# Ten wo chunks on chip, zeros in other places, and part of the last w1 stage summed on VectorE

## The chip, the core and the metric

The kernel runs on one core of a Trainium2 chip. It is one launch. The metric is the device time of the whole program in microseconds, the median of several executions; before the change it is 450.8 us (five runs, 448.94 to 454.15). A core has a matrix engine (PE, with a separate row for its weight loads, PEld), a vector engine (DVE), a scalar engine (ACT), a general engine (POOL) and a sync engine (SP). SP and POOL issue the DMA transfers; all transfers run on the core's 16 DMA engines.

## The reference

A decoder of four layers works on a single token: x is one row of 1024 numbers. Attention and MLP alternate, and both kinds share their weights between the two layers of the kind.

```python
x = x + A(layernorm(x)); x = x + B(layernorm(x))
x = x + A(layernorm(x)); x = x + B(layernorm(x))
# A: q = x @ wq; scores over the last W = 4096 of 32768 cached keys, softmax,
#    times the cached values, @ wo.  32 heads of 128, 4 key/value heads
# B: h = x @ w1 + b1; act = h * tanh(softplus(h)); act @ w2.  1024 -> 3584 -> 1024
```

The outputs are x and, for a given grad_out, the gradients of everything but B_x: of x, of the two caches (32768 positions each, of which only the last 4096 have a gradient that is not zero), of wq (1024 x 4096), wo (4096 x 1024), w1 (1024 x 3584), b1 and w2 (3584 x 1024), all in bfloat16. The zeros of the two cache gradients alone are 58.7 MB of the 98.6 MB that are written.

## The kernel before

A single token makes every weight matrix a matrix-vector product, so the kernel is a sequence of passes over the weights. In order: attention forward (called A1), MLP forward (B2), attention forward again (A3), then the second MLP, which is run forward and backward in one pass over w1 (`mlp_turn`, B4), then attention backward (A3), a pass over w2 that serves the second MLP's forward product and the first MLP's backward product at once (`W2Pass.rest`), the first MLP's backward product with w1 (`mlp_bwd_w1`), and attention backward (A1). The outer products that make the weight gradients come last, when all vectors are known.

wq, K, V and the first NR = 9 chunks of wo stay on chip. A chunk of wo is 256 rows, 0.524 MB; there are 16. The other seven chunks, all of w1 (16 chunks of 0.459 MB, or 14 blocks of 0.524 MB in `mlp_turn`) and all of w2 (14 chunks of 0.524 MB) are loaded anew for each pass into NB = 6 stream buffers, tag `st` of the pool `strm`. A load is issued by SP as soon as its buffer is free, and SP issues in program order: a load that waits for its buffer holds back every later one. The seventh wo chunk of a pass always has to wait for one of the six buffers. In the second forward attention the order of the chunks is the first streamed one, the nine kept ones, the other six (line 541); in the backward attentions the seventh is loaded inside `T` (line 807).

A backward attention needs wo @ g. For the kept chunks 0 to 7 the product runs on rows of the kept, already transposed copy (line 835); the ninth uses `bwd_rows2`. For each streamed chunk half of the rows are transposed on PE (`xpose`), copied back and multiplied, and half are summed on VectorE against g broadcast over the partitions (line 813, g in PSUM as `gbc`, made by `bcast_row`). Each `xpose` puts up to eight transposes into a PSUM tile and copies them out; `evac` gives the copy to VectorE or ScalarE by a running estimate of both. `fill` transposes pieces of wo, V, K and wq in place where PE has time, in that order of the keys; these copies are needed later.

`mlp_bwd_w1` does a full transpose of each w1 chunk (14 blocks of 128 columns) and 14 products, the products one chunk behind the transposes (`pipe`).

The zeros are 112 transfers of 0.524 MB from one tile of zeros, `zt`. `bg_zeros(n, after)` puts a small copy on POOL that waits for the vector `after`, and n zeros behind it; POOL's queue is in order and at most eight of its transfers are outstanding. `zeros(n)` puts them on SP's queue. The table `Z` (line 1133) says how many go where: 3 near the end of the first w2 pass, 16 in the second forward attention, 5, 2, 1, 2, 1, 2 and 6 at the seven blocks of `mlp_turn`, 6 and 26 in the first backward attention, 3 at the last w1 stage, 3 at the start and 36 (on SP) in the last backward attention.

`warm(n)` issues n matmuls of no use whose result is thrown away. `hooks` places pieces of the coming w2 pass into gaps of the layer norm's backward step: "copy" after the copy of the row, "sel" after the sums that follow, "ln" after the norm's sum.

## Time and profile before

| | us |
|---|---|
| median of 5 runs | 450.8 (448.94 to 454.15) |
| the profiled execution, its own time | 449.98 |
| its span in the profile | 447.9 |
| PE, DVE, ACT, POOL busy | 321.8, 236.8, 225.0, 56.8 |
| moved by the DMA engines | 172.25 MB, mean 385 GB/s |

The span is what the profile covers; the remaining 2.1 us lie around it. Busy times are per engine and overlap. The page's second part cuts the span into 40 slices of 11.2 us and gives for each the share of busy time of every engine, the clock of PE (PEclk, in tenths of full speed), the busy share of the DMA engines and the GB/s that they moved. The third part lists the DMA queues: q1 is SP's, q0 is POOL's. The trace can also be asked for the same figures in any other stretch, for the instructions in order of time, and for the transfers in a stretch with their packet sizes. In the timeline an instruction's line holds its start, its time, the engine, the line of the kernel, the operation, what it writes and reads, and in brackets how long the engine had been idle before it and what ended that.

### The profile page before, as it was taken

Reading aid. Unit: us, or ns where it says so; the run is one execution under the profiler, and the core shown is the slowest. Engines: PE = TensorE matmul, PEld = TensorE weight load, DVE = VectorE, ACT = ScalarE, POOL = GpSimd, SP = SyncE. Lnnn points to the kernel's source line nnn. Section 1 sums busy time; section 2 is a strip of 40 time slices with the busy share of each in tenths; the row PEclk is TensorE's granted clock in tenths of the full one; section 3 lists DMA queues with packets and bytes.
Section 4 is the critical chain, followed back from the end, with each engine's and each line's share of the span. In section 5 each row is a group of like instructions: output and inputs, shape, how many; then the busy total and the mean of one; then the engine's idle time right before and its main releaser. Section 6 shows DMA issues by size and latency. Waiting matters only on the chain.

```text
span 447.9 us, 11941 instructions
## 1 busy us (share of the span) xinstructions
PE 321.8 (72%) x5107; PEld 216.7 (48%) x5107; DVE 236.8 (53%) x489; ACT 225.0 (50%) x262; POOL 56.8 (13%) x146
## 2 busy tenths in 40 slices
PE   0556755488997989977799688778868669897400
PEld 0333524387466979954797677754531111121000
DVE  3134201187332756773265855483259889999600
ACT  1121200075241857875493454445329899989600
POOL 2000000001431311341341020052010000000000
PEclk9998555578876999998798589999785555555555
DMA  8999998999999998999999899999999999999994
GB/s 319 393 409 423 409 409 297 408 343 324 417 415 393 395 376 301 384 412 415 416 415 404 320 330 370 341 367 418 416 416 419 419 416 417 418 417 420 416 417 169
DMA packets 52257, 172.25 MB, mean 385 GB/s; under 512 B 5200, under 2 KB 12396, under 8 KB 51180
## 3 DMA queue, kind: packets, MB, share of 16 engines
q1 hardware_dynamic: 41120, 131.61, 75.4%
q0 software_dynamic: 11040, 39.86, 22.2%
q8 instruction: 40, 0.66, 0.6%
q14 instruction: 13, 0.11, 0.1%
q10 hardware_dynamic: 44, 0.01, 0.0%
HBM read 72.89 MB, written 98.58 MB: 383 GB/s over the span
## 4 chain that ended last, share of the span: by engine, by line
PE 20%; ACT 13%; DMA 8%; issue 5%; DVE 4%; POOL 1%; DVEq 0%; ACTq 0%; SPq 0%; POOLq 0%
PE ops L229 6%; DMA w_c<-in_B_w_dram 6%; PE tps L193 6%; ACT wq_b L148 6%; PE acc L229 3%; ACT wo_b L148 2%; DMA wo_c<-in_A_wo_dram 2%; ACT st_o L148 2%; ACT K L148 2%; ACT wo_c L148 1%; PE d L229 1%; DVE K L145 1%; PE tps L623 1%; ACT V L148 1%; PE sm L229 1%
## 5 line engine op out<-in xcount | busy, mean ns | idle before, releaser
L138 POOL DMA_DIRECT2D out_dram<-zt x76 | 40.6, 537 | 44.4 <-DMA out_dram<-zt 41.9
L229 PEld LDWEIGHTS <-w_c 128*128 128x128 bf16 x1120 | 35.8, 101 | 18.9 <-DMA w_c<-in_B_w_dram 14.5
L633 ACT COPY w_c<-tps 128x1024 bf16<-128x1024 bf16 x28 | 28.3, 1012 | 21.6 <-PE tps L623 12.0
L229 PE MATMUL ops<-V 2*128 2x512 bf16 (+1 forms) x160 | 34.8, 598 | 5.9 <-ACT wq_b L148 3.4
L647 DVE CUSTOM_DVE_ANT_0 scr<-w_c,gbc 128x1024 bf16<-128x1024 bf16 x28 | 34.2, 1221 | 5.4 <-DMA w_c<-in_B_w_dram 3.4
L145 DVE CAST wq_b<-ops 128x1024 bf16<-128x1024 f32 (+1 forms) x31 | 33.8, 1149 | 3.8 <-PE ops L229 3.2
L148 ACT CAST wq_b<-ops 128x1024 bf16<-128x1024 f32 (+1 forms) x33 | 33.7, 1138 | 2.2 <-PE ops L229 2.0
L148 ACT COPY K<-tps 128x1024 bf16<-128x1024 bf16 x19 | 18.6, 1029 | 28.4 <-PE tps L193 28.4
L229 PE MATMUL ops<-wo_b 2*128 2x512 bf16 x120 | 23.3, 567 | 10.9 <-ACT wq_b L148 7.2
L229 PEld LDWEIGHTS <-V 128*128 128x128 bf16 (+2 forms) x416 | 14.0, 100 | 27.8 <-issue 27.6
L229 PE MATMUL q<-wq_b,nA_pair 128*32 128x512 bf16 x128 | 11.6, 447 | 16.8 <-DMA wq_b<-in_A_wq_dram 16.8
L623 PE MATMUL tps<-ident_bf,w_c 128*128 128x128 bf16 x224 | 22.3, 260 | 0.6 <-DMA w_c<-in_B_w_dram 0.6
L148 ACT COPY w_b<-tps 128x1024 bf16<-128x1024 bf16 x20 | 19.5, 1015 | 5.5 <-PE tps L193 4.7
L145 DVE COPY K<-tps 128x1024 bf16<-128x1024 bf16 x13 | 8.8, 689 | 24.9 <-PE tps L193 23.0
L229 PEld LDWEIGHTS <-wo_b 2*128 2x128 bf16 (+1 forms) x152 | 5.6, 99 | 29.2 <-issue 28.6
L813 DVE CUSTOM_DVE_ANT_0 wo_c<-wo_c,gbc 128x1024 bf16<-128x1024 bf16 x14 | 16.4, 1218 | 6.0 <-DMA wo_c<-in_A_wo_dram 4.3
L193 PE MATMUL tps<-ident_bf,w_c 128*128 128x128 bf16 x224 | 16.4, 231 | 4.2 <-DMA w_c<-in_B_w_dram 4.2
L229 PE MATMUL acc<-a_pair,w_c 128*128 128x16 bf16 x448 | 15.6, 171 | 5.1 <-DMA w_c<-in_B_w_dram 5.0
L148 ACT COPY w_c<-tps 128x768 bf16<-128x768 bf16 (+1 forms) x14 | 11.6, 830 | 14.7 <-PE tps L193 13.7
L148 ACT CAST K<-ops 128x1024 bf16<-128x1024 f32 x18 | 17.7, 1014 | 2.5 <-PE ops L229 1.8
L193 PE MATMUL tps<-ident_bf,wq_b 128*128 128x128 bf16 x256 | 17.6, 235 | 1.5 <-issue 1.5
L148 ACT COPY wq_b<-tps 128x1024 bf16<-128x1024 bf16 x16 | 15.2, 1043 | 6.6 <-PE tps L193 6.6
(323 smaller groups left out, 660.8 us busy)
## 6 DMA issues: line engine op xcount, KB each, us to landing
out_dram<-zt POOLq DMA_DIRECT2D x76, 512.0 KB, 10.6
out_dram<-zt SPq DMA_DIRECT2D x36, 512.0 KB, 8.5
wo_c<-in_A_wo_dram SPq DMA_DIRECT2D x28, 512.0 KB, 7.8
w_c<-in_B_w_dram SPq DMA_DIRECT2D x32, 448.0 KB, 6.6
w_c<-in_B_w_dram SPq DMA_DIRECT2D x28, 512.0 KB, 6.8
out_dram<-wq_b SPq DMA_DIRECT2D x17, 512.0 KB, 11.5
wq_b<-in_A_wq_dram SPq DMA_DIRECT2D x16, 512.0 KB, 11.8
out_dram<-K SPq DMA_DIRECT2D x8, 1024.0 KB, 12.8
```

The source lines that it names most:

```text
L138: nc.gpsimd.dma_start(zero_jobs.pop(0), zt[:])
L145: nc.vector.tensor_copy(out_ap, in_ap)
L148: nc.scalar.copy(out_ap, in_ap)
L193: nc.tensor.transpose(ps[:, b, :], ap, ident_bf[:])
L229: nc.tensor.matmul(out_ap, lhsT=lhsT, rhs=rhs, start=start, stop=stop, skip_group_check=True, **kw)
L623: nc.tensor.transpose(self.ps[c][:, b, :], w[:, 1, b * P:(b + 1) * P], ident_bf[:])
L633: nc.scalar.copy(self.w[c][:, 1, :], self.ps.pop(c)[:].rearrange("p b c -> p (b c)"))
L647: nc.vector.tensor_tensor_reduce(out=scr[:], in0=w[:, 0, :], in1=gbc[:], scale=1.0, scalar=0.0, op0=ALU.mult, op1=ALU.add, accum_out=self. ...
L813: nc.vector.tensor_tensor_reduce(out=w[:, 0, :], in0=w[:, 0, :], in1=gbc[:], scale=1.0, scalar=0.0, op0=ALU.mult, op1=ALU.add, accum_out=w ...
```

## The change

NR goes from 9 to 10, so ten chunks of wo stay on chip and six are streamed. The room comes from smaller helpers: the tile of zeros is halved and read twice by a broadcast, the matrix of 1/D becomes a column that is broadcast, the pattern matrix `pat` is replaced by four narrow matmuls with `fold`, the replicated q and do columns are kept once instead of four times, and two small tiles share a place with others. The second forward attention takes its first three streamed chunks before the kept ones. `Z` is written anew, with two new places in the first MLP, several in one w2 pass, and one in the second w2 pass. In the first MLP the broadcast of g is made after four w1 chunks instead of before the first. In the last w1 stage columns 0 to 1023 of each even chunk are no longer transposed and multiplied on PE; VectorE multiplies them with dh, broadcast over the partitions in PSUM, and sums them. The hooks get warm matmuls and one w2 chunk less.

```diff
-NR = 9
+NR = 10
...
-    onesD = keep.tile([P, P], FP32, name="onesD")
-    nc.vector.memset(onesD[:], invD)
+    ones1 = keep.tile([P, 1], FP32, name="ones1")
+    nc.vector.memset(ones1[:], invD)
+    onesD = ones1[:, 0:1].to_broadcast([P, P])
...
-    zt = keep.tile([P, ZC], BF16, name="zt")
+    zt = keep.tile([P, ZC // 2], BF16, name="zt")
     nc.gpsimd.memset(zt[:], 0.0)
+    zt2 = zt[:, None, :].to_broadcast([P, 2, ZC // 2])
...
-                zero_jobs.append(zflat[:, i * ZC:(i + 1) * ZC])
+                zero_jobs.append(zflat[:, i * ZC:(i + 1) * ZC].rearrange("p (a b) -> p a b", a=2))
...
-            nc.sync.dma_start(zero_jobs.pop(0), zt[:])
+            nc.sync.dma_start(zero_jobs.pop(0), zt2)
...
+    def over_groups(out, rhs, start, stop):
+        for c in range(NC):
+            mm(out[32 * c:32 * c + 32, :], fold[:], rhs, start, stop, tile_position=(0, 32 * c))
...
-        nc.vector.tensor_copy(tt[:, 0:TD], dn_ps)
+        if more is None:
+            nc.vector.tensor_copy(tt[:, 0:TD], dn_ps)
+        else:
+            nc.vector.tensor_add(tt[:, 0:TD], dn_ps, more)
...
-        order = early + late if first else late[0:1] + early + late[1:]
+        order = early + late if first else late[0:3] + early + late[3:]
...
-            if not first and i == 0:
-                held[NO - 1] = wo_load(NO - 1)
...
-        gbc = bcast_row(g_bf)
         for i in range(2 * TD):
             t, hf = i // 2, i % 2
             w = w1_load(i)
+            if i == 4:
+                gbc = bcast_row(g_bf)
+                bg_zeros(Z["B2a"], n_bf)
...
+        def blocks(i):
+            return range(8 if i % 2 == 0 else 0, NW2)
+
         def T(i):
             w = w1_load(i)
             ws[i] = w
-            xpose(*alt_blocks(w[:, 0:1024], 4))
+            if i % 2:
+                xpose(*alt_blocks(w[:, 0:1024], 4))
             xpose(*alt_blocks(w[:, 1024:1792], 3))
...
+        def V(i):
+            if i % 2 == 0:
+                ev[0] += 1.3
+                nc.vector.tensor_tensor_reduce(out=ws[i][:, 0:1024], in0=ws[i][:, 0:1024], in1=big[0][:], scale=1.0, scalar=0.0,
+                                               op0=ALU.mult, op1=ALU.add, accum_out=tw[:, i // 2:i // 2 + 1])
...
-        pipe(list(range(2 * TD)), T, M)
-        return ln_bwd(nacc.cols(0, TD), sv["n32"], sv["rstd"], g_col, lname, nxt)
+        rep8 = work.tile([P, TD, P], BF16, name="rep8", tag="kp")
+        nc.vector.tensor_copy(rep8[:], sv["dh_bf"][:, 0:TD, None].to_broadcast([P, TD, P]))
+        T(0)
+        top("two")
+        big.append(pools["top"].tile([P, D], FP32, name="dhbc"))
+        for k in range(TD):
+            o = (k // 2) * 2 * P + k % 2
+            mm(big[0][:, o:o + 2 * P - 1:2], rep8[:, k, :], ident_bf[:], k % 4 == 0, True)
+        V(0)
+        for i in range(1, 2 * TD):
+            T(i)
+            V(i)
+            M(i - 1)
+        M(2 * TD - 1)
+        return ln_bwd(nacc.cols(0, TD), sv["n32"], sv["rstd"], g_col, lname, nxt, tw[:])
...
-        bwd_rows2(dacc, wo_kept[NR - 1], NR - 1, g_bf, started=False)
+        for c in range(8, NR):
+            bwd_rows2(dacc, wo_kept[c], c, g_bf, started=c > 8)
...
-    Z = dict(B2=3, A3=16, B4=[5, 2, 1, 2, 1, 2, 6], A3c=6, A3d=26, W1=3, A1c=3, A1d=36)
+    Z = dict(B2a=2, B2={0: 2, NW2 - 2: 3}, A3=17, B4=[1, 2, 2, 2, 2, 2, 3], A3c=6, A3d=24, B4w={2: 2}, W1=4, A1c=3, A1d=37)
...
-    hooks.update(copy=lambda: w2p.tp(0), sel=lambda: w2_ahead([0]), ln=lambda: w2_ahead([1, 2]))
+    def copy_gap():
+        w2p.tp(0)
+        warm(3)
+
+    def sel_gap():
+        w2_ahead([0])
+        warm(2)
+
+    def ln_gap():
+        w2_ahead([1])
+        warm(4)
+
+    hooks.update(copy=copy_gap, sel=sel_gap, ln=ln_gap)
     g2, g2b = attn_bwd(g3, g3b, "A3", sA3, True, "B2")
-    x4, wg2 = w2p.rest(3, g2b, x3, "x_B4", bcast_row(g2b), 0)
+    x4, wg2 = w2p.rest(2, g2b, x3, "x_B4", bcast_row(g2b), Z["B4w"])
```

The new `Z` asks for 114 zeros and there are 112, so the last run on SP has 35.

## The prediction

> **What bounds the kernel now.** I read the page's slices first, because the kernel moves 172 MB and I wanted to know whether the transfers leave any room.
>
> ```profile
> GB/s 319 393 409 423 409 409 297 408 343 324 417 415 393 395 376 301 384 412 415 416 415 404 320 330 370 341 367 418 416 416 419 419 416 417 418 417 420 416 417 169
> ...
> q0 software_dynamic: 11040, 39.86, 22.2%
> ...
> HBM read 72.89 MB, written 98.58 MB: 383 GB/s over the span
> ```
>
> The best slices hold 416 to 420 GB/s; I take 417 as the ceiling, so a 0.524 MB transfer costs 1.26 us where the queues are full. From slice 28 (302 us) to the end all slices but the last are at the ceiling: what counts there is how many bytes are left. Before it are dips, and there the chain of work decides. So I need two accounts: the chain up to the point P where the last w1 stage has written gA_pair (291.9 us), and the bytes after P.
>
> Next, stretches of 2 us around the dips (time; busy us of PE, PEld, DVE, ACT, POOL; PEclk; DMA share; GB/s).
>
> ```profile
> 70.00:72.00 2.00, 1.04 (x15) 1.04 (x16) 0.90 (x3) 0.00 (x0) 0.00 (x0) 0.50 0.54 206
> 72.00:74.00 2.00, 2.00 (x82) 2.00 (x79) 0.00 (x0) 0.00 (x0) 0.00 (x0) 0.50 0.43 61
> 136.00:138.00 2.00, 0.87 (x32) 0.78 (x32) 0.69 (x1) 0.00 (x0) 0.00 (x0) 1.00 1.04 422
> 162.00:164.00 2.00, 0.56 (x16) 0.47 (x16) 0.55 (x1) 0.47 (x1) 0.00 (x0) 1.00 1.09 365
> 172.00:174.00 2.00, 2.00 (x57) 2.00 (x55) 1.71 (x5) 0.31 (x2) 0.00 (x0) 1.00 0.41 154
> ```
>
> At 70 to 74 the six stream buffers are full and the queues empty; at 136 and 162 it is the reverse, full queues and an idle PE; at 172 PE is full and the queues empty. Zeros that sit in the second kind and not in the first are in the wrong place. The timeline names what PE waited for, the seventh streamed wo chunk (139, 202) and a late w1 chunk (286):
>
> ```profile
> 139.15 0.59 PE L229 MATMUL sm<-o_pair,wo_c 128*128 128x16 bf16 x16 [2.27 <-DMA wo_c<-in_A_wo_dram]
> ...
> 202.70 0.62 PE L193 MATMUL tps<-ident_bf,wo_c 128*128 128x128 bf16 x8 [1.41 <-DMA wo_c<-in_A_wo_dram]
> ...
> 286.45 0.96 PE L193 MATMUL tps<-ident_bf,w_c 128*128 128x128 bf16 x14 [1.33 <-DMA w_c<-in_B_w_dram]
> ```
>
> SP's own timeline shows the same seventh load ahead of the last run of zeros:
>
> ```profile
> 289.86 5.75 SPq L348 DMA_DIRECT2D wo_c<-in_A_wo_dram  x2
> 295.66 6.03 SPq L129 DMA_DIRECT2D out_dram<-zt  x4
> ```
>
> **The change, along the chain.** With ten chunks kept, six are streamed, and the six buffers hold all of them: the seventh load, which waited for a buffer and then for the zeros ahead of it, is gone from three stages (three loads of 0.524 MB).
>
> *Second forward attention (112 to 142).* PE's 2.27 us wait goes; its matmuls and the 13 row chunks stay. The seventeenth zero (one more) lies behind, in a queue that is full either way. -2.3.
>
> *Second MLP, forward and back (144 to 190).* PE is 2.00 of 2.00 almost throughout; it idled 0.15 + 1.44 + 0.50 us at 160 to 166 for a w1 block behind ten zeros. The zeros go from 5, 2, 1, 2, 1, 2, 6 to 1, 2, 2, 2, 2, 2, 3: two w1 blocks (1.05 MB at 348 GB/s, 3.0 us) and two zeros (2.5 us) fit in the 6.4 us of a block. I take 1.5 of the 2.1 us. Five zeros fewer leave holes here, which cost the chain nothing. -1.5 (0 to -2.1).
>
> *First backward attention (190 to 242).* The 1.41 us wait goes. Chunk 9 costs 16 products from the kept copy (0.55) where its streamed form cost 8 transposes and 8 products (0.62 + 0.36): -0.4. Against it, two more kept chunk halves were transposed in the MLP's fixed slots, so two K units slide into this stage, 8 transposes at 0.57 to 0.61 each: +1.2. Together -0.7. The three hooks get nine warm matmuls; at full clock 512 columns take about 0.22 us (7 in 1.67 us at 290). Those at "copy" and "sel" stand ahead of the next step on PE, less what the DVE copy hides: +0.65; the four at "ln" take the place of chunk 2's forward products and transposes. The broadcast after them ran at clock 0.50 (1.04 us, 0.62 at full clock), so I give 0.35 back: +0.3.
>
> *First MLP (70 to 110).* Moving the broadcast behind four w1 chunks lets PE start 1.6 us earlier at 70.2; two zeros (2.5 us) enter the hole at 71 to 74.5. The w1 loads then end about when they did; the broadcast (1.03 us) hides beside them, PE being half idle at 76 to 80, and would cost that if it were not. Two zeros at w2's first chunk: DVE sets the pace there (1.22 + 0.08 us each of 14), six buffers ahead; +0.5 for a load that comes late (0 to +2.5).
>
> *Second w2 pass (243 to 264).* Two zeros more, but its backlog is shorter by two zeros and a wo load (3.8 us) against a chain shorter by 0.7. DVE's waits for loads there are 0.17 + 0.77 + 0.68; 0 (-1 to +1.5).
>
> *Last w1 stage (264 to 290).* A pair of chunks cost 28 transposes and 28 products, 2.27 us of PE; now 20 and 20, 1.62. DVE per pair: one 768-column copy (0.56) and the new sum over 1024 columns (1.22 + 0.08, the row of the same operation in the w2 stage) = 1.86; ACT 1.01 + 0.80 = 1.81. At 0.93 us a chunk both lie under the load (0.459 MB, 1.1 us): no engine becomes the bound. What it adds on the path is the broadcast of dh: 0.69 (DVE) + 1.03 (PE), beside the first transposes. Before, the stage took 1.5 us a chunk, with waits for loads that land 6.4 to 7.5 us after issue. Now the loads decide: chunks 6 to 15 (4.6 MB) and four zeros (2.1 MB) from 266.3 take 16.1 us; +2 for landing and +2.4 for the last chunk's transposes, eviction and products make 286.8 against 289.8. Six buffers held 2.4 us each keep it from reaching that: -2.5 (0 to -5). VectorE runs in order: behind each sum stands the next 768-column copy, and PE's products wait for that, with 0.2 us of slack a chunk.
>
> *After P.* From 291.9 to 447.9 it is 156.0 us. One zero fewer remains (38 for 39): -1.26. The wo load: -1.26. SP's zeros no longer stand behind it, up to 5.8 us earlier; the stretches from 290 to 302 lack 0.69 MB against 417 GB/s (1.7 us), of which I take 1.2. -3.7.
>
> Chain -6.2, bytes -3.7. Can the queues follow? Before P 110.4 MB move now (172.25 less 61.8, the stretches after P added up); two wo loads fewer and one zero more make 109.9 MB, 263.6 us at 417, plus 3.3 at the start and 3.7 for the 1 KB rows: 270.6 of 285.7 us. The holes shrink from 20 to 15 us; it can. At no cost: the small sums of the softmax (four narrow matmuls for one of 0.39 us) and the row layouts, which lie where ACT and DVE end at 421 us and the transfers at 441.
>
> **The zeros' source.** It is halved, and a broadcast makes each row two runs of 2 KB instead of one of 4 KB. No row shows 2 KB. The two sides, the w1 blocks (1 KB rows) and the last stores:
>
> ```profile
> DMA packets 1391, 1.39 MB, mean 348 GB/s; under 512 B 46, under 2 KB 1390, under 8 KB 1390
> ...
> DMA packets 1368, 4.99 MB, mean 416 GB/s; under 512 B 150, under 2 KB 150, under 8 KB 1368
> ```
>
> So 1 KB takes 47 ns on a DMA engine and 4 KB 158; a straight line gives 84 for 2 KB, +0.08 us a zero. But 3.5 KB rows (360 to 376 us) hold 416 too, so the surcharge fades before 4 KB. I take half, 0.04: 38 zeros after P, 1.5 us; 47 in the full stretches before it, 1.9, of which 0.5 reaches the chain. +2.0. The ends: none, 0; at the 1 KB price, +0.25 a zero.
>
> [...]
>
> **The sum.** -6.2 - 3.7 + 2.0 = -7.9 on the profiled execution's own 449.98 us (span 447.9 and 2.1 around it): 442. The median is 450.8, so that is 2% faster.
>
> **Rivals.** *More of it:* 2 KB costs nothing and the w1 stage reaches its load rate (-3.0 or better), second w2 pass -1: 449.98 - 6.2 - 3.7 - 1.5 - 2 = 436.5. For it: 3.5 KB rows pay nothing. Chance 0.18. *Only bytes:* the waits return elsewhere (17 zeros ahead of the first w1 blocks, zeros ahead of w2 loads); three loads (3.8 us) go, 2 KB eats 2, 1 KB rows as before: 448, from 446.3 to 453. For it: the w2 loads at 244 took 6.9 us behind zeros. 0.20, most of it within 1%. *The change does not do what it says:* zeros gated at 70 start too late for the hole (the first buffer came free at 72.1 and the rate was back only in 74 to 76, so some 2 us pass from issue to bytes) and lengthen the w1 loads by 2.5: 444.5, within the forecast. *Slower:* zeros at the 1 KB price. The place is the runs where only zeros flow (112 to 140, 200 to 240, 295 on): 85 of the 112 outside the thin stages, 0.25 each, 21 us in place of 2: 461. It decides from 0.12 us a zero (+9%), where 85 zeros eat the 9.9. Against it: the same 4 KB is written in order. 0.12.
>
> Chances: 442 (438 to 446) 0.50, 436 0.18, bytes only 0.20, slower 0.12. Beyond 1%, about what a measurement can tell from no change (446.3 to 455.3): faster 0.69, same 0.19, slower 0.12. The range takes in most of the neighbours on both sides: 435 to 453.
>
> **What would show it.** Zero-only stretches at 417 GB/s (no surcharge), 404 (mine) or 348; no wait for wo_c in the last chunks of any attention stage; no PE hole at the fourth block of the second MLP; 70 to 74 above 300 GB/s; P near 285; the last w1 stage about 25 us from dh to P instead of 27.6, its sums at 1.22 us. It is wrong if P moves by less than 3 us, or if the stretch after P grows.

## The result, and the profile after

The changed kernel takes **455.0 us** (median of 22 runs, 452.3 to 459.0) against 451.2 us of the kernel before in the same comparisons: ratio **1.0082**, 95% interval 1.0057 to 1.0106. It is 0.8% slower where 2% faster was forecast, and 455 lies outside the range of 435 to 453. The profiled execution took 457.31 us, with a span of 455.2. (Of the runs below, the profile of e7 is of an execution in a slower state, at a granted clock of 0.717, so no stage is read from it.)

The page of the changed kernel, the same lines as before:

```profile
GB/s 321 389 414 413 406 408 343 411 389 340 397 401 371 319 336 368 350 361 407 412 373 261 362 286 347 325 374 402 392 380 379 404 405 403 402 406 400 407 407 323
...
q1 hardware_dynamic: 45024, 129.52, 75.0%
q0 software_dynamic: 11184, 40.39, 23.2%
...
HBM read 71.31 MB, written 98.58 MB: 373 GB/s over the span
```

The bytes fell as the sum said (71.31 MB read for 72.89), but the *rate* fell more, to 373 GB/s for 383. Two things are new. From slice 28 on, where only stores are left, all slices but the last stand at 379 to 407 where they stood at 416 to 420. And slices 22 to 26, the second w2 pass and the last w1 stage, run thinner than before: 261 to 362 where they stood at 320 to 404.

The stretches of the prediction, and two new ones at 148 and 248 us (time; busy us of PE, PEld, DVE, ACT, POOL; granted clock; DMA share; GB/s):

```profile
70.00:72.00 2.00, 1.63 (x58) 1.63 (x58) 1.08 (x3) 0.00 (x0) 1.62 (x3) 0.50 0.75 260
72.00:74.00 2.00, 1.68 (x37) 1.59 (x34) 0.00 (x0) 0.00 (x0) 0.72 (x1) 0.50 0.91 235
136.00:138.00 2.00, 2.00 (x37) 0.82 (x30) 0.00 (x0) 0.00 (x0) 0.69 (x1) 0.91 1.00 369
148.00:150.00 2.00, 0.00 (x0) 0.00 (x0) 0.00 (x0) 0.00 (x0) 0.00 (x0) 0.50 1.04 353
162.00:164.00 2.00, 2.00 (x57) 2.00 (x55) 1.56 (x9) 1.71 (x3) 0.00 (x0) 1.00 1.07 400
248.00:250.00 2.00, 1.90 (x56) 1.73 (x53) 1.97 (x3) 1.65 (x3) 0.00 (x0) 1.00 0.50 135
```

The old holes are closed as meant: 61 GB/s became 235 at 72, and PE is full at 136 and at 162. But at 148 PE does nothing at all beside a full queue, and at 248 the queue is half empty beside a full PE. The timeline says what PE waits for at 147 and 150:

```profile
147.02 0.60 PE L231 MATMUL sm<-nB_pair,w_b 128*128 128x16 bf16 x16 [2.75 <-DMA w_b<-in_B_w_dram]
150.46 0.59 PE L231 MATMUL sm<-nB_pair,w_b 128*128 128x16 bf16 x16 [2.85 <-DMA w_b<-in_B_w_dram]
```

The wait for the seventh wo chunk is gone, and its heir is the first w1 block of the turn. The chain can be taken from gate to gate (GpSimd's small copies that release the zeros, the broadcast of g at the start of the second w2 pass, and VectorE's operation that writes dh, the gradient that the first MLP's w1 product needs). The gates at the ends of the table's first, second and fifth row, before and then after:

```profile
112.52 0.19 POOL L136 COPY gate_t<-nA_pair 128x1 bf16<-128x1 bf16 x1 [2.45 <-DVE nA_pair L295]
...
189.72 0.19 POOL L136 COPY gate_t<-gA_pair 128x1 bf16<-128x1 bf16 x1 [5.87 <-DVE gA_pair L321]
...
291.98 0.64 POOL L136 COPY gate_t<-gA_pair 128x1 bf16<-128x1 bf16 x1 [24.38 <-DVE gA_pair L321]
```

```profile
115.79 0.19 POOL L138 COPY gate_t<-nA_pair 128x1 bf16<-128x1 bf16 x1 [2.67 <-DVE nA_pair L301]
...
194.14 0.19 POOL L138 COPY gate_t<-gA_pair 128x1 bf16<-128x1 bf16 x1 [7.92 <-DVE gA_pair L330]
...
300.76 0.64 POOL L138 COPY gate_t<-gA_pair 128x1 bf16<-128x1 bf16 x1 [24.96 <-DVE gA_pair L330]
```

So the chain moved like this:

| stretch | before, us | after, us | forecast | measured |
|---|---|---|---|---|
| start to nA gate (first MLP and before) | 112.52 | 115.79 | +0.5 | +3.3 |
| nA gate to gA gate (second attention, turn) | 77.20 | 78.35 | -3.8 | +1.2 |
| gA gate to second w2 pass | 52.33 | 51.73 | -0.4 | -0.6 |
| second w2 pass to dh | 21.82 | 24.78 | 0 | +3.0 |
| dh to P | 28.11 | 30.11 | -2.5 | +2.0 |
| P to the end of the span | 155.9 | 154.4 | -3.7 and +1.5 | -1.5 |

P is at 300.76 instead of 291.98: +8.8 us for a forecast of -6.2 (and +0.5 of the zeros' price).

### The profile page after: what moved, and what is told of

It is laid out like the page before. It is cut to its first block, busy times and chain, and to the rows that moved or that the text cites. A ratio compares the mean times of both kernels' runs of the same rounds, so it can differ in the third digit from the quotient of the medians.

```text
span 455.2 us, 11790 instructions
## 1 busy us (share of the span) xinstructions
PE 325.7 (72%) x5060; PEld 221.1 (49%) x5060; DVE 237.1 (52%) x491; ACT 227.4 (50%) x264; POOL 72.6 (16%) x150
## 3 DMA queue, kind: packets, MB, share of 16 engines
HBM read 71.31 MB, written 98.58 MB: 373 GB/s over the span
## 5 line engine op out<-in xcount | busy, mean ns | idle before, releaser
L140 POOL DMA_DIRECT2D out_dram<-zt x77 | 56.2, 731 | 33.0 <-DMA out_dram<-zt 27.1
L150 ACT COPY K<-tps 128x1024 bf16<-128x1024 bf16 x20 | 19.4, 1024 | 30.3 <-PE tps L195 30.3
L147 DVE CAST wq_b<-ops 128x1024 bf16<-128x1024 f32 (+1 forms) x29 | 31.7, 1151 | 3.6 <-PE ops L231 3.0
L150 ACT CAST wq_b<-ops 128x1024 bf16<-128x1024 f32 (+1 forms) x31 | 31.7, 1137 | 2.2 <-PE ops L231 2.0
L231 PEld LDWEIGHTS <-V 128*128 128x128 bf16 (+2 forms) x416 | 14.1, 101 | 27.8 <-issue 27.6
L630 PE MATMUL tps<-ident_bf,w_c 128*128 128x128 bf16 x224 | 22.6, 262 | 0.8 <-DMA w_c<-in_B_w_dram 0.8
L150 ACT COPY w_c<-tps 128x1024 bf16<-128x1024 bf16 (+1 forms) x16 | 13.7, 908 | 14.6 <-PE tps L195 10.8
L195 PE MATMUL tps<-ident_bf,K 128*128 128x128 bf16 x256 | 19.5, 236 | 0.0
L195 PEld LDWEIGHTS <-K 128*128 128x128 bf16 x256 | 16.6, 107 | 4.2 <-issue 4.1
```

What stands on the lines that cost most here:

```text
L140: nc.gpsimd.dma_start(zero_jobs.pop(0), zt2)
L147: nc.vector.tensor_copy(out_ap, in_ap)
L150: nc.scalar.copy(out_ap, in_ap)
L195: nc.tensor.transpose(ps[:, b, :], ap, ident_bf[:])
L231: nc.tensor.matmul(out_ap, lhsT=lhsT, rhs=rhs, start=start, stop=stop, skip_group_check=True, **kw)
L630: nc.tensor.transpose(self.ps[c][:, b, :], w[:, 1, b * P:(b + 1) * P], ident_bf[:])
```

## The experiments

Two suspects came out of the two traces. One is the **places** of the zeros: those that now stand ahead of loads. The other is the **rate** of the transfers themselves, which fell even where the bytes and their form are the same. The sum on VectorE is the third thing to settle.

### e1: the old places

```diff
-Z = dict(B2a=2, B2={0: 2, NW2 - 2: 3}, A3=17, B4=[1, 2, 2, 2, 2, 2, 3], A3c=6, A3d=24, B4w={2: 2}, W1=4, A1c=3, A1d=37)
+Z = dict(B2a=0, B2={NW2 - 2: 3}, A3=16, B4=[5, 2, 1, 2, 1, 2, 6], A3c=6, A3d=26, B4w={}, W1=3, A1c=3, A1d=36)
```

> The changed kernel with the zero transfers gated where the kernel before had them (3 at w2 chunk 12, 16 in the second forward attention, 5 2 1 2 1 2 6 in the turn, 26 in the first backward attention, 3 at the last w1 stage, none in the second w2 pass). Theory 'places' (the gain went to zeros that now stand ahead of loads: first MLP +1.7, first w2 pass +1.6, first block of the turn +5.2 against the 4.7 gained before it, second w2 pass +3.0): those waits go, nB gate near 140, start of the second w2 pass 3 to 4 us earlier, P about 294 to 296 instead of 300.8, the time about 449 (ratio to the kernel before about 0.995). Theory 'end of the queue' (what is after P decides, two-run rows and slower stores): P may come earlier, but the queue is full from the start of the last w1 stage on and the time stays within 2 us of 455. Against both: 5 zeros at the turn's first block are more than the 1 of the change; if the sum ahead of that block decides (16 + 5 for 17 + 1), the turn's first block becomes longer still, by 2.5 to 4 us.

Measured: 451.8 us, ratio 0.9985 (0.9950 to 1.0020); the changed kernel's 1.0082 lies outside that. P came at 296.65, 4.1 us earlier. The nA gate is back at 112.52, so the 3.3 us of the first MLP are the zeros at 70 and at w2's first chunk, and nothing else. The turn's first block takes 6.5 us again, but its third took 10.5. The waits of PE from 138 us to the turn's end (us in total, times, longest), the changed kernel and then e1:

```profile
PE sm L231 <- DMA w_b<-in_B_w_dram: 5.6, 2, 2.8
```

```profile
PE sm L231 <- DMA w_b<-in_B_w_dram: 6.1, 4, 4.1
```

In the kernel before it was 2.1. So the hole only moved: zeros issued in the second attention and in the turn meet the w1 loads one block earlier or later.

One wait stayed. E1 puts no zeros into the second w2 pass, and yet the pass took 25.0 us to dh, where the changed kernel took 24.8. VectorE waited there for loads, and when the pass began (243 us) the queue was still full of GpSimd's zeros, at 359 to 381 GB/s from 238 to 248 us:

```profile
253.48 1.22 DVE L654 CUSTOM_DVE_ANT_0 scr<-w_c,gbc 128x1024 bf16<-128x1024 bf16 x1 [1.99 <-DMA w_c<-in_B_w_dram]
...
255.42 1.22 DVE L654 CUSTOM_DVE_ANT_0 scr<-w_c,gbc 128x1024 bf16<-128x1024 bf16 x1 [0.71 <-DMA w_c<-in_B_w_dram]
...
258.90 1.22 DVE L654 CUSTOM_DVE_ANT_0 scr<-w_c,gbc 128x1024 bf16<-128x1024 bf16 x1 [2.25 <-DMA w_c<-in_B_w_dram]
```

### e2: the old last w1 stage

```diff
-        T(0)
...
-        V(0)
-        for i in range(1, 2 * TD):
-            T(i)
-            V(i)
-            M(i - 1)
-        M(2 * TD - 1)
+        pipe(list(range(2 * TD)), T, M)
```

> The changed kernel with the last w1 stage of the kernel before: all 14 blocks of every chunk on TensorE, no sum on VectorE and no broadcast of dh. Theory 'VectorE sum costs' (broadcast 1.9 us at half the granted clock, and a thinner TensorE stage in which the granted clock stays at 0.50): the stage from dh to P shrinks from 29.7 to about 27.6, the granted clock is 1.00 in its second half, the time falls by 1 to 2 us, to 453 to 454. Theory 'loads decide' (my forecast's own step): the stage grows by 1 to 2.5 us with TensorE back at 1.6 us a pair more, time 456 to 458. Third: it makes no difference, under 1 us, because the four zeros and the loads of the stage set its length.

Measured: 456.0 us, ratio 1.0066 (1.0026 to 1.0107): the same as with the sum. From dh to the layer norm's first copy the stage took 27.6 us, with the sum 27.95. In e1, with the sum but three zeros, it took 25.96; the kernel before, without the sum and with three zeros, 25.95. The stage is longer in the kernels with the fourth zero, whichever engine sums. The profiles read here part this way: 24.7 to 26.6 us with three zeros (the kernel before, e1, e4, e6, e8, e9, e11, e14, e15, e16), 27.2 to 27.95 with four (the changed kernel, e2, e3, e5, e13). But the kernels with four also have the other new places, and no run moves that one zero alone.

### e3 and e4: one run of 4 KB, or two of 2 KB

In e3 SyncE's late zeros read a 4 KB row again, from a slot of the stores; in e4 the kernel before gets the halved source, and nothing else.

```diff
 # e3, on the changed kernel
-        slots.extend(cut_up(wo_flat, 8192, (2048,) * (NR - 4)))
+        *sl, zl = cut_up(wo_flat, 8192, (2048,) * (NR - 4))
+        slots.extend(sl)
+        nc.gpsimd.memset(zl, 0.0)
 # e4, on the kernel before
-    zt = keep.tile([P, ZC], BF16, name="zt")
+    zt = keep.tile([P, ZC // 2], BF16, name="zt")      # and zt2, as in the change
```

> The changed kernel whose 35 zeros on SyncE's queue after P read one run of 4 KB a row again, from a buffer of 4 KB that is one store slot fewer (5 slots there, as the kernel before). The zeros that GpSimd issues keep the two runs of 2 KB. Theory '2 KB packets on SyncE's queue cost' (304 to 352 us at 379 to 401 GB/s instead of 416): the packets of that stretch are 4 KB, its rate 415 or more, and the time falls by 3 to 4.5 us, to 451 or 452. Theory 'the whole end is slower for another reason' (the stores behind it too run at 399 to 410 GB/s): the rate stays at 380 to 405 and the time stays within 1 us of 455. By my forecast's price of 0.04 us a zero it would fall by 1.4.

> The kernel before with one edit: the zero source is half as wide and a broadcast makes each row two runs of 2 KB. Theory '2 KB packets on SyncE's queue cost, on GpSimd's not': the 36 zeros after P take 0.1 to 0.13 us more each, the time rises by 3.5 to 4.5 us to 454.5 to 455.5 (ratio 1.008 to 1.010); the stretches where only GpSimd's zeros flow (112 to 140, 205 to 238) keep 415 GB/s and 4 KB packets. By my forecast's price (0.04 a zero, on both queues): +2.0. By the price of 1 KB rows: +20. If the stores after 352 us also fall from 416 to about 405 GB/s here, the slower end of the changed kernel comes with the zeros' form too.

Measured: e3 456.2 us, 1.0081 (1.0048 to 1.0115); e4 453.7 us, 1.0036 (0.9988 to 1.0085), not told apart from no change. E3's windows show why its time says little: the zeros waited for the memset and began 10 us later than in the changed kernel (309.05 for 299.01 us on SyncE's queue), which left a hole.

```profile
304.00:312.00 8.00, 4.72 (x76) 3.70 (x69) 5.02 (x9) 3.26 (x5) 5.25 (x14) 0.83 0.53 208
312.00:320.00 8.00, 6.82 (x95) 4.33 (x97) 1.03 (x5) 5.83 (x8) 2.85 (x18) 0.96 1.02 402
...
384.00:400.00 16.00, 14.09 (x80) 2.94 (x80) 15.04 (x14) 15.28 (x17) 0.00 (x0) 0.50 1.02 402
```

But they also show something I had not thought of: with 4 KB rows the zeros run at 402, not 416, and so do the stores at 384 that no edit touched. In e4, on the other base, zeros of two 2 KB runs hold 404 to 406 GB/s at 304 to 344 and the stores behind them 417 to 419:

```profile
312.00:320.00 8.00, 6.83 (x71) 3.32 (x70) 4.52 (x18) 2.14 (x3) 1.07 (x6) 1.00 1.05 404
...
352.00:368.00 16.00, 9.35 (x53) 1.77 (x52) 13.50 (x14) 13.98 (x14) 0.00 (x0) 0.50 1.03 418
```

Zeros and stores of the kernel before, and then of the changed kernel:

```profile
328.00:336.00 8.00, 4.19 (x44) 2.44 (x37) 3.98 (x13) 2.46 (x3) 1.67 (x6) 0.84 1.03 416
...
352.00:368.00 16.00, 9.58 (x52) 1.81 (x52) 12.75 (x13) 13.93 (x14) 0.00 (x0) 0.50 1.03 418
```

```profile
328.00:336.00 8.00, 6.28 (x137) 3.72 (x134) 0.00 (x0) 1.30 (x3) 0.07 (x1) 0.68 1.04 379
...
352.00:368.00 16.00, 12.10 (x60) 2.40 (x56) 15.66 (x15) 15.18 (x16) 0.00 (x0) 0.50 1.03 403
```

So in e4 two runs of 2 KB cost 3% (404 for 416 GB/s), 0.04 us a zero; and the changed kernel has a second slowness, in transfers of any form, that e4 does not have.

### e5 and e6: 32 bytes

What else differs is where the buffers lie in SBUF. In the kernel before the zero source starts at a multiple of 512 bytes and K and V 256 past one; in the changed kernel these are 32 and 288, and wq and wo are at 64 instead of 32.

```diff
 # e5, on the changed kernel: everything behind lies 32 bytes lower
-    ones1 = keep.tile([P, 1], FP32, name="ones1")
-    eps_t = keep.tile([P, 1], FP32, name="eps_t")
+    one_eps = keep.tile([P, 2], FP32, name="one_eps")
+    ones1, eps_t = one_eps[:, 0:1], one_eps[:, 1:2]
 # e6, on the kernel before: the same with eps_t and sel2
```

> The changed kernel with two small constants (1/D and eps) in one tile, so that every buffer behind them lies 32 bytes lower in SBUF: zero source, K and V at multiples of 64 bytes, wq, wo and the stream buffers at 32 past one, as in the kernel before (in the changed kernel it is the other way round). Nothing else differs. In the profiles the 4 KB packets of SyncE's stores take 159.6 to 161 ns in the kernel before and its two-run variant and 163 to 165 ns in the changed kernel and three variants of it. Theory 'address' (the 64-byte position of the buffers sets the packet time): packets back to about 160, the stretch from 352 us to the end at 416 to 420 GB/s instead of 399 to 410, the V loads at 159, the time falls by 5 to 8 us, to 447 to 450 (ratio 0.985 to 0.997). Theory 'program' (number of slots, order of stores, DRAM placement of the program): packets stay at 163 to 165, time 455 within 1 us.

> The kernel before with two small constants (eps and the row selector) in one tile, so that every buffer behind them lies 32 bytes lower: zero source, K and V at 32 past a multiple of 64 bytes, wq, wo and the stream buffers at multiples of 64, as in the changed kernel. Theory 'address': the store packets of 4 KB go from 160 to 163 to 165 ns, the stores at the end run at about 404 GB/s, the time rises by 6 to 10 us, to 458 to 462. Theory 'program': 160 ns and about 452 as before.

Measured: e5 451.3 us, 0.9990 (0.9959 to 1.0021). One tile less, 32 bytes, and some 4 us are back. P came at 298.1 and the rest took 152.3 us, 2.2 less than in the changed kernel. Its zeros on SyncE's queue run at 403 to 407 GB/s for 379 to 392 (320 to 344 us), its stores at 405 to 420:

```profile
336.00:344.00 8.00, 3.28 (x29) 2.53 (x33) 3.55 (x16) 1.01 (x1) 1.17 (x5) 0.76 1.05 407
...
352.00:368.00 16.00, 11.17 (x60) 2.18 (x58) 14.59 (x15) 14.51 (x14) 0.00 (x0) 0.50 1.03 419
```

But e6 went against the simple form of the theory: 450.1 us, 0.9957 (0.9921 to 0.9994), not slower at all. Its wq loads (at a multiple of 512 there) even became faster, 159 ns a packet for 163, while part of its stores went from 160 ns to between 161 and 165. "The other side of 64 bytes" is not the rule.

### e7, e8, e9: both cures together

e7 has the edits of e1 and e5; e8 besides these the old last w1 stage; e9 is e7 with three zeros moved from the second forward attention to the first backward one (`A3=13`, `A3d=29`).

> The changed kernel with both cures at once: zeros gated where the kernel before has them, and every buffer 32 bytes lower. Theory 'two causes' (places cost about 4 us, the 32 bytes about 4, independent of each other): P near 293 to 295, the stretch after P about 152, time 446 to 448 (ratio 0.985 to 0.993). Theory 'one cause' (both let the same full queue catch up before P): the gains overlap, time 450 to 451.5 as with either alone.

> The kernel with both cures, and the last w1 stage of the kernel before (no sum on VectorE). So far the stage from dh to the layer norm's first copy took 25.95 us (kernel before, 3 zeros, all on TensorE), 25.96 (sum on VectorE, 3 zeros), 27.6 (TensorE, 4 zeros), 27.5 and 27.95 (VectorE, 4 zeros). Theory 'loads and zeros set the stage, whichever engine sums': 26 us again, time within 0.3% of the kernel with both cures. Theory of my forecast (the sum takes 2.5 us off): stage 28 to 28.5, time 2 us longer. Theory 'the sum costs' (a wait for ScalarE's copies in place of the wait for loads): stage 24.5 or less, time 1 to 1.5 us shorter.

> The kernel with both cures, with three zeros moved from the second forward attention (13 for 16) to the first backward one (29 for 26). Theory 'zeros ahead of the w1 loads': in the changed kernel with the old places the third block of the turn took 10.5 us against 4.9 to 5.3, TensorE idle for w1 blocks that stand beside zeros; three fewer ahead of them take 3.8 us off that wait, and three more behind lie over the stretch at 246 to 250 us where the queues run thin. nB gate the same or 1 us earlier, end of the turn 2 to 4 us earlier, P 1.5 to 3 us earlier, time 1.5 to 3 us less than with both cures alone. Theory 'the queue is full anyway': the second w2 pass starts behind three zeros more, P and time within 1 us.

| kernel | us | ratio to the kernel before |
|---|---|---|
| changed kernel | 455.0 | 1.0082 (1.0057 to 1.0106) |
| e1, old places | 451.8 | 0.9985 (0.9950 to 1.0020) |
| e5, 32 bytes lower | 451.3 | 0.9990 (0.9959 to 1.0021) |
| e7, both | 447.2 | 0.9885 (0.9860 to 0.9911) |
| e8, both, no sum on VectorE | 448.1 | 0.9910 (0.9873 to 0.9948) |
| e9, both, three zeros later | 445.6 | 0.9853 (0.9807 to 0.9899) |

The gains add up: 0.0097 and 0.0092 alone, 0.0197 together. So there are two causes, not one seen twice. E9's interval does not part it from e7, but its trace shows the step: the wait for w1 blocks, 6.1 us in e1, is no longer among the turn's waits, and the turn takes 44.9 us from gate to gate (45.6 before, 51.4 changed):

```profile
140.31 0.18 POOL L138 COPY gate_t<-nB_pair 128x1 bf16<-128x1 bf16 x1 [14.21 <-DVE nB_pair L301]
...
185.17 0.19 POOL L138 COPY gate_t<-gA_pair 128x1 bf16<-128x1 bf16 x1 [6.80 <-DVE gA_pair L330]
```

P is at 288.9.

### e10 and e12: loads and zeros alone

Here the offset is measured by itself, without a kernel around it.

```diff
+    for c in range(16):                         # e12: offset 0 everywhere
+        at = 10240 + 2560 * c + (0, 32, 64, 256)[c // 4] // 2
+        nc.sync.dma_start(big[:, at:at + 2048], wo_v[c])
+    for order in (offs, (288, 0, 448, 64, 256, 32, 480, 128, 320, 96, 384, 192)):
+        for o in order:
+            for k in range(4):
+                nc.sync.dma_start(dst.pop(0), big[:, 2560 * k + o // 2:2560 * k + o // 2 + 2048])
```

> No layer is computed and only the zeros are written. Sixteen 4 KB-row loads of wo go to SBUF rows that start 0, 32, 64 and 256 bytes past a multiple of 512 (four loads each), then 96 transfers of zeros with 4 KB rows are issued by SyncE from rows 0, 32, 64, 96, 128, 192, 256, 288, 320, 384, 448 and 480 bytes past a multiple of 512, four each, once in this order and once in another, then sixteen of two 2 KB runs from 0 and 32. Theory 'the 64-byte position of a buffer sets its own packet time': odd multiples of 32 give 163 to 165 ns in both passes, the others 159 to 160, whichever pass; two runs of 2 KB 84 from 0 and 86 to 89 from 32. Theory 'not the buffer's own position' (only the whole kernel's mix of buffers): 159 to 160 throughout, in both passes; then the 32 bytes act through something that this kernel does not have.

> The kernel of loads and zeros alone, with every row at offset 0 (a multiple of 512 bytes), all else the same. In the run with mixed offsets the first 48 stores took 159 ns a packet at every offset, and from the 49th on 161 to 167 with 159 again for offsets 0 and 256 at first. Theory 'destination or time' (the second output, or how long the queue has run): the second half is at 161 to 167 here too. Theory 'offsets, by way of the packets before' (rows off the 512-byte grid bring the engines out of step, rows on it bring them back): 159 to the end, the two-run rows at 84, and 420 GB/s throughout.

The packet records of e10's second pass, mean duration of a 4 KB packet, in the order of issue:

```
offset past 512   288    0   448    64   256    32   480   128   320    96   384   192
ns              161.5  159.0 161.5 163.5 159.0 160.7 163.7 163.9 164.0 163.9 163.9 167.5
```

In the first pass all twelve took 159.0 or 159.1. The loads tell little (159 to 163, the first group with the start of the queue in it). The rates of e10 (time; GpSimd; clock; DMA share; GB/s): first pass, second pass, two runs of 2 KB from offset 32:

```profile
48.00:68.00 20.00, 0.00 (x0) 1.00 1.03 420
...
112.00:132.00 20.00, 0.00 (x0) 1.00 1.02 406
...
160.00:164.00 4.00, 0.00 (x0) 1.00 1.03 381
```

And of e12, the same transfers to the same places with every row at offset 0:

```profile
112.00:132.00 20.00, 0.00 (x0) 1.00 1.03 420
...
160.00:162.00 2.00, 0.00 (x0) 1.00 1.05 409
```

E12 holds 159 ns and 420 GB/s to the end of its 4 KB rows, so neither the destination nor the time slows the queue: the offsets do (each of the two kernels ran once). They don't do it at once, though. Twelve offsets ran at full pace as long as none had slowed; once the queue was slow, only the rows at 0 and 256, the two of the twelve on a grid of 256 bytes, were at 159. Why the price comes late is not shown. Rows of two 2 KB runs ran at 409 GB/s on the grid, for 420 with 4 KB (0.035 us a zero), and at 381 off it, the rate of the changed kernel's late zeros (379 to 381).

In these two runs a start off the grid cost 0 to 4.5% of the rate for 4 KB rows (420 down to 401 GB/s, e10 at 132 to 146 us) and 7% for two runs of 2 KB (409 to 381). What in the transfer takes that time no run shows.

### e11 and e14: the sum on VectorE, in order

e9's waits of PE in this stage, then those of e11, in which the copies are dealt out by hand (of an odd chunk ScalarE 1024 columns and VectorE 768, of an even one ScalarE the 768); e14 is e9 without the sum.

```diff
 # e11, in T(i)
-                xpose(*alt_blocks(w[:, 0:1024], 4))
-            xpose(*alt_blocks(w[:, 1024:1792], 3))
+                xpose(*alt_blocks(w[:, 0:1024], 4), "a")
+            xpose(*alt_blocks(w[:, 1024:1792], 3), "v" if i % 2 else "a")
```

> The kernel with both cures and three zeros moved later, and in the last w1 stage the copies are dealt out by hand: of an odd chunk ScalarE takes the 1024 columns and VectorE the 768, of an even one ScalarE the 768 while VectorE sums. So far ScalarE took both copies of each odd chunk one after the other (1.71 us), TensorE waited for it, and VectorE took the even chunk's. Theory 'the new wait on ScalarE ate the gain': the stage from dh to the next layer's gate goes from 26.85 us to 24.5 to 25.5, the time falls by 1 to 2 us. Theory 'loads set it' : 26.5 to 27, time the same within 0.3%. By my forecast's sum (0.93 us of either engine a chunk, loads of 1.1 us): 24.4 or less.

> The kernel with both cures and three zeros moved later, and the last w1 stage all on TensorE. With both cures the stage from dh to the layer norm took 24.9 us in this form, with the sum on VectorE 26.6, with the sum and the copies dealt out by hand 24.7. Theory 'the sum as written costs': stage near 24.9, time 1 to 2 us less than 445.6. Theory 'the queue evens it out' (a stage that ends earlier finds the transfers no further): time the same within 0.3%, as between the two kernels with both cures (0.9885 and 0.9910).

PE's waits in the stage: the kernel before, e9, and e11 (us in total, times, longest):

```profile
PE tps L193 <- DMA w_c<-in_B_w_dram: 4.2, 5, 1.6
```

```profile
PE acc L231 <- ACT w_c L150: 3.6, 11, 0.7
...
PE tps L195 <- DMA w_c<-in_B_w_dram: 1.2, 2, 1.0
```

```profile
PE tps L195 <- DMA w_c<-in_B_w_dram: 3.3, 3, 1.7
...
PE acc L231 <- ACT w_c L150: 1.3, 3, 0.7
```

The sum: 4.2, 4.8 and 4.6 us. The sum on VectorE does take work off PE, and the wait for loads shrinks; but a wait for ScalarE comes in its place, because the helper that balances the copies gives ScalarE both copies of every odd chunk (1.71 us in a row). With the copies dealt out by hand, most of the wait for loads is back. From dh to the layer norm's copy the stage took 26.6 us in e9, 24.7 in e11, and 25.8 (e14) and 24.9 (e8) with no sum at all. The times don't part: e9 0.9853, e11 0.9884 (0.9805 to 0.9963), e14 0.9876 (0.9793 to 0.9959). The step is worth nothing, in either direction, that these runs can tell.

### e13, e15, e16: which buffers

e13 moves the zero source alone onto a multiple of 512. e15 (on e9) and e16 (on the kernel before) order the buffers so that stream buffers, zero source, wq, wo, K and V all start at multiples of 256; nothing grows.

```diff
 # e15, e16
+    small = ctx.enter_context(tc.tile_pool(name="small", bufs=1))   # x0, eps_t, sel2, neg1: 128 bytes
+    strm = ctx.enter_context(tc.tile_pool(name="strm", bufs=NB))
     keep = ctx.enter_context(tc.tile_pool(name="keep", bufs=1))
     work = ctx.enter_context(tc.tile_pool(name="work", bufs=1))
-    strm = ctx.enter_context(tc.tile_pool(name="strm", bufs=NB))
+    ...                                                             # zt, wq_b, wo_b, K, V first in keep
```

> The changed kernel with the zero source alone 32 bytes lower, on a multiple of 512 (it and the 512-byte identity change places with a 32-byte tile); wq, wo, K, V and the stream buffers stay where the changed kernel has them. Theory 'the zero source': the 35 zeros after P run at 404 GB/s instead of 381 (2.5 us), and the stores behind them, no longer started out of step, at 412 to 420 instead of 399 to 410 (1.5 to 2.5 us more): 450.5 to 452.5, as when all buffers were moved. Theory 'all buffers': zeros at 404, stores still at 399 to 410: 452.5 to 453.5. Theory 'the step is lost anyway': zeros still at 380 to 390, 455.

> The kernel with the old zero places and three zeros later, with its buffers laid out in another order so that the stream buffers, the zero source, wq, wo, K and V all start at a multiple of 256 bytes (nothing grows; in the kernel before zero source, K and V do, in the changed kernel none). In the run of mixed offsets only the groups at 0 and 256 kept 159 ns a packet once the queue had slowed. Theory 'rows on 256 bytes keep the packets short': loads of wq, V and wo at 159 to 160 ns instead of 162 to 164, all stores after P at 159 to 160, 418 to 421 GB/s after the zeros, time 2 to 4 us below the 445.6 of the same kernel 32 bytes lower (ratio 0.975 to 0.982). Theory 'only the zero source counts' : packets of loads and stores as there, time within 1 us of it.

> The kernel before with the same order of buffers, all of them at multiples of 256 bytes; nothing else differs. Theory 'rows on 256 bytes keep the packets short': loads of wq and wo at 159 to 160 ns instead of 163 to 164 (some 12 MB of them ahead of the chain, 0.7 us), stores flat as they are, time 0.5 to 2 us shorter (ratio 0.995 to 0.999). Theory 'only the zero source counts' (it is on 512 already): no change.

Windows of the changed kernel, of e13, and of e15:

```profile
336.00:344.00 8.00, 5.34 (x74) 3.22 (x73) 3.33 (x12) 1.69 (x2) 1.17 (x5) 0.89 1.04 381
...
384.00:400.00 16.00, 14.12 (x84) 2.87 (x78) 15.05 (x14) 15.17 (x17) 0.00 (x0) 0.50 1.02 402
```

```profile
336.00:344.00 8.00, 4.80 (x63) 3.38 (x52) 3.66 (x14) 1.52 (x2) 1.17 (x5) 0.84 1.05 406
352.00:368.00 16.00, 11.81 (x57) 2.32 (x56) 14.73 (x15) 15.18 (x16) 0.00 (x0) 0.50 1.03 419
...
384.00:400.00 16.00, 14.10 (x80) 2.86 (x74) 15.04 (x14) 15.27 (x17) 0.00 (x0) 0.50 1.00 401
```

```profile
44.00:64.00 20.00, 13.52 (x207) 6.86 (x207) 2.58 (x10) 2.18 (x6) 0.00 (x0) 0.52 1.03 418
...
384.00:400.00 16.00, 14.27 (x76) 2.97 (x74) 16.00 (x15) 14.95 (x17) 0.00 (x0) 0.50 1.03 420
```

E13: 453.4 us, 1.0004 (0.9957 to 1.0051), better than the changed kernel. Its zeros hold 406, and the stores from other buffers, still off the grid, start at 419 behind them and fall to 401 later on. So the zero source is part of the 4 us; the rest of e5's gain came with the other buffers, which e5 moved as well. E15: 444.8 us, **0.9809** (0.9767 to 0.9852); e16: 449.1 us, **0.9941** (0.9907 to 0.9975). In both every load of wq, V and wo takes 159 to 161 ns a packet once the queue is running (162 to 164 in the changed kernel, and for wq and wo in the kernel before too), 422 GB/s at 24 to 44 us for 414 and 417, and the stores to the end 159 to 161 (163 to 166 in the changed kernel). The loads of the changed kernel, of the kernel before, and of e15:

```profile
24.00:44.00 20.00, 12.37 (x165) 7.51 (x164) 6.98 (x14) 5.43 (x9) 0.00 (x0) 0.91 1.02 414
```

```profile
24.00:44.00 20.00, 12.11 (x157) 6.84 (x156) 6.48 (x12) 4.75 (x6) 0.00 (x0) 0.91 1.02 417
```

```profile
24.00:44.00 20.00, 12.43 (x165) 7.78 (x164) 6.95 (x14) 5.45 (x9) 0.00 (x0) 0.91 1.02 422
```

A grid of 256 bytes fits all these runs, on both kernels. E15's interval overlaps e9's, so its gain over e9 stands in the packets and not in the time; e16's over the kernel before stands in both. E15 beats both kernels, by 1.9% and 2.7%.

## Why the prediction was wrong

**First MLP, +0.5; measured +3.3.** The step said that two zeros enter the hole at 71 to 74 and "the w1 loads then end about when they did". The zeros did fill the hole (235 GB/s for 61), and the loads behind ended later: against e1, which differs in the places alone, VectorE's first sum of the w2 pass starts 2.8 us later (91.15 for 88.31) and the nA gate comes 3.3 later. So most of the delay is there when the second pair of zeros is released; no run parts the two pairs. Moving the broadcast was right: in e1 the same sum starts 1.3 us earlier than in the kernel before (89.61), though waits for w2 loads had eaten that by the nA gate. The range allowed +2.5. My own rival had named the cause for the first pair (gated too late, bytes 2 us behind the issue) and priced it at 2.5; I counted it as inside the forecast.

**Second forward attention, -2.3, and turn, -1.5; together +1.2.** The wait for the seventh chunk went, and the stage became 4.7 us shorter. The failing step is one sentence, that the seventeenth zero "lies behind, in a queue that is full either way". In this stage the full queue (369 GB/s at 136, 353 at 148) was not a place where a zero cost nothing. The w1 blocks of the turn were next in it: PE waited 2.75 and 2.85 us for the loads of the first, and from the nA gate to the end of the turn's first block it took 37.9 us before and 38.4 after: one wo load had gone out of that queue and one zero of the same 0.524 MB had come in. The four zeros fewer at the turn's own gate were no relief, since those in the way are the 17 ahead. From the nA gate to the gA gate the kernels with 13 zeros there (e9, e11, e14, e15) take 72.7 to 75.0 us, those with 16 or 17 take 76.6 to 80.7.

**First backward attention, -0.4; measured -0.6.** Right as a sum; its parts were not measured one by one.

**Second w2 pass, 0 (-1 to +1.5); measured +3.0.** I compared a shorter backlog with a shorter chain. The chain came 3.8 us later, the zeros before it had run out, and the queue was half empty (135 GB/s at 248) when the pass started; then two more zeros stood beside its loads. VectorE waited 4.3 us for loads in this pass, 1.6 before. But the two zeros alone are not the cause: e1 has none there, and took 25.0 us for 24.8. E5, with the zeros and 32 bytes lower, took 22.9; e8, without them and 32 bytes lower, 19.7; e9, e11, e14 and e15, which let three more zeros loose before it, 23.1 to 24.6. So the zeros released before the pass and their rate count as well, and no run parts the three.

**Last w1 stage, -2.5; measured +2.0.** Half of the step was right: no engine became the bound by its busy time. The loads "decide", and they decided against it: the stage takes 24.7 to 26.6 us to the layer norm's first copy in the kernels with three zeros and 27.2 to 27.95 in those with four. And the sum on VectorE gains nothing: PE had been waiting for loads before, and the time taken off PE came back as waits (4.2 us before, 4.8 and 4.6 in e9 and e11). My arithmetic also spread the 1.81 us a pair evenly, 0.93 us a chunk, where ScalarE did both copies of the odd chunk in one go. I let the chunks come at the pace of the queue; as I read the trace, the pace is that of six buffers with a landing time of 5 to 6.4 us each (median of the stage's w1 loads: 6.4 in the kernel before, 5.1 in the changed one, 5.0 in e1). The broadcast that I priced at 1.03 us took 1.89 at clock 0.50.

**After P, -3.7 +1.5; measured -1.5.** The net -2.2 lies between what two runs show. In e5 the rest takes 152.3 us, -3.6 against the kernel before with the price of 2 KB included, but there P comes 6 us later, so more had been moved ahead of it; in e9, with P at 288.9 and one zero more behind it, it takes 154.7, -1.2. What the changed kernel loses here against e5, and against e13 with the zero source alone moved (152.4), is where the buffers start.

**The zeros' source, 0.04 us a zero; measured 0.035 to 0.04 on the grid** (409 for 420 alone, 404 for 416 in e4). Right in size, though half of the straight line was a guess: the packets alone took 84.0 ns on the grid (e10, e12), as the line had it, and the rate fell by half of that. But the changed kernel's source is not on the grid, and there a zero on SyncE's queue took 1.376 us for 1.257, +0.12. GpSimd's zeros remained 4 KB packets. They paid nothing for long stretches (416 GB/s at 116 to 124 us) and much in others: where they flow alone, at 229 to 237 us, in the changed kernel, in e13, and in the kernel before:

```profile
229.00:237.00 8.00, 8.00 (x145) 8.00 (x143) 6.08 (x9) 8.00 (x10) 4.76 (x7) 1.00 1.01 369
```

```profile
229.00:237.00 8.00, 8.00 (x146) 8.00 (x143) 6.13 (x9) 7.73 (x10) 4.65 (x7) 1.00 1.03 410
```

```profile
229.00:237.00 8.00, 8.00 (x147) 6.11 (x143) 4.15 (x6) 5.39 (x6) 3.19 (x6) 1.00 1.03 417
```

The change of the addresses was in no part of the sum: I read the halved tile as a change of form and not as one that moves every buffer behind it. That term is worth 4 us (e5), and the places another 4 (e1). Without both the kernel is 1.1% faster than the one before (e7), and 1.5% with three zeros moved as well (e9), so the forecast of 2% would have been nearer; but that is another kernel, without the new places that were to bring part of it.

Of the rivals, "only bytes" came closest in kind (the waits return elsewhere), with 448, up to 453, and no term for the rate. The slower rival had the right direction, and its threshold of 0.12 us a zero is what SyncE's 35 zeros paid (it counted 85); but its reason, the length of the runs, is worth 0.035 to 0.04 of that, and where they start is the rest. The sum of *more of it* takes off 2.0 us that -6.2 and -3.7 do not hold; without them it is 438.5.

## What to carry to other kernels

In these kernels, whose DMA engines were busy 8 or 9 tenths in 39 of the page's 40 slices, background stores had a price wherever a load was next: with 13 zeros in the second forward attention it took 72.7 to 75.0 us from the nA gate to the gA gate, with 16 or 17 it took 76.6 to 80.7. So put them where the next load is farthest, and count, for each, which load lands behind it. Where a buffer changes size, list the addresses of all buffers behind it: here one tile less, 32 bytes, was worth some 4 us (e5), and on the kernel before a start at a multiple of 256 bytes for the rows that DMAs read or write was worth 0.6% by itself (e16). Work taken off an engine that waits for loads can go into that wait, as in the last w1 stage here (4.2 us of waits before, 4.8 and 4.6 with the sum in e9 and e11); look first at what the wait would be then.

## What the hardware did that I had not expected

- 32 bytes of SBUF address were worth 0.9% of this kernel (e5 against the changed kernel: 0.9990 for 1.0082). In e10 rows off the 256-byte grid ran at 159 ns a 4 KB packet for the first 48 transfers and at 161 to 167 later, while those on the grid were back at 159; in e13 the stores off the grid ran at 419 GB/s right behind the zeros on it, and at 401 some 30 us later.
- Two runs of 2 KB a row became packets of 2 KB where SyncE issued them and of 4 KB where GpSimd did: the changed kernel's q1 has 3904 packets more for 2.1 MB less, and q0's grew only with its bytes (144 more for 0.53 MB more).
- A GpSimd zero took 731 ns to issue with the broadcast source, 537 before; it hid behind the transfers, since GpSimd still waited 27.1 us in all for zeros to land (41.9 before).
- In the changed kernel the last w1 stage ran at a granted TensorE clock of 0.55 to 0.60 from 282 to 294 us, where it was 1.00 before, and 14 transposes took 1.68 us instead of 0.96. The sum on VectorE is not what did it: e2, with all blocks on TensorE, had 0.51 at 282 to 288, and e1, with the sum, 0.92 to 0.93 at 282 to 294. What did is open.
